# First attention: four query groups in one batch on 64-row halves, and a part of the keys' sums on ScalarE

## The chip, the cores and the metric

The kernel runs on one core of one Trainium2 chip. The metric is the device time of one execution in microseconds (us). The engines of the core work beside each other, each in the order of its own instructions, and wait for each other by semaphores: TensorE (PE in the profile; PEld is its loading of weights), VectorE (DVE), ScalarE (ACT), GpSimd (POOL) and SyncE (SP), which here only issues transfers (DMAs).

## The reference: two attentions and two MLPs in turn

The input x has 2048 tokens of 576 features, in bfloat16. Four layers are run, each added to x after a layer norm of its own: attention, MLP, attention, MLP, both attentions with the same weights and both MLPs too.

```python
qkv = (x @ wqkv) ...                      # 32 heads of 18 features
phi = lambda t: jnp.where(t > 0, t + 1, jnp.exp(t)) + 1e-6
pq, pk = phi(q), phi(k)
kv = jnp.einsum("bhsd,bhse->bhde", pk, v)
z = jnp.einsum("bhsd->bhd", pk)
num = jnp.einsum("bhqd,bhde->bhqe", pq, kv)
den = jnp.einsum("bhqd,bhd->bhq", pq, z)[..., None] + 1e-6
o = num / den                             # then o @ wo
```

The attention is linear: the keys and values are summed over all tokens into one small matrix per head, and the queries are multiplied with it. The MLP is 576 to 4608 with gelu and back; its input is normed twice, once by the layer and once inside.

## The kernel before

Tokens are in 16 tiles of 128; four tiles are a block of 512. The normed input is kept transposed in `yT`, five chunks of 128 features by 2048 tokens: four full chunks and a fifth with 64 features in its upper 64 rows; in the first attention the lower 64 rows of that chunk hold padding, against which the weights are zero. TensorE's order is the order in which the code calls `mm`, and the other engines are also held to the order of the code (the classes `InOrder` at L48 and the helper at L53, so that almost every row of the profile names L53 or L229).

**phi of a projection.** A projection lands in PSUM in float32. phi is computed as max(t, 0) + (min(exp(t), 1) + 1e-6). For a group of queries ScalarE reads PSUM twice (exponential and relu, 512 columns), and VectorE later clamps and adds the two in bfloat16 (`q_sum`). These sums are put in a list, `q_late`, and `finish(n)` does the oldest n of them.

**The key tiles of the first attention** (the loop over `t in range(NT)` in `layer_A`). At tile t TensorE transposes the normed tile t + 2, projects the keys of tile t + 1 in two halves (`k_half`, 288 columns, the second with 72 columns of values beside it), and between the matmuls of the second half does five small products with the sums `pk` of tile t (`m_side`); then four matmuls of 504 columns add the tile to the products of input and keys (`m_main`). ScalarE copies the transposed tile, takes the exponential of each half (`phi_e`) and copies the values. VectorE norms a tile further ahead, takes the statistics of one beyond that, and then does `k_finish`: for each half a clamp of `phi_e` (TENSOR_SCALAR) and a sum with the positive part, read from PSUM (SCALAR_TENSOR_TENSOR). GpSimd computes the reciprocal standard deviations and makes the masks, one batch a tile, each after that tile's last key sum. At seven tiles (1, 2, 3, 5, 7, 10, 14) one of the 18 query groups is projected between the second and the third of the four matmuls. PSUM banks one0, one1 and one2 go round among transposes, key halves and queries; the side products stay in one3.

**Behind the key tiles** the products are folded with the value and output weights (`kv_wo`), the first block's denominators are made, and five more query groups are projected. `kv_wo(4)` puts four small copies on SP. Then the output of the first block's four tiles is computed (`wo_stage`): VectorE adds it to x and takes the statistics of the next norm; ScalarE norms the first two tiles, VectorE the last two, and TensorE transposes them. Six query groups are projected among these: behind the first and the second output tile, and four after the last one, the very last with the fourth transposes between its second and third matmul. A query group (`q_next`, `q_proj`) is five matmuls of 128 rows by 512 columns; the fifth group of a pair of blocks, with 72 of the features, is 20 matmuls of 64 columns each way.

**The MLP's first matmuls follow.** `groups(2, ...)` runs two groups of the first MLP's hidden features for block 0, on the upper and the lower 64 rows of the array at the same time (`row_tiles`): each row half works on its own PSUM bank, and halves change banks in turns through a relay. Behind them come the denominators of the other blocks, which need all query sums.

**The second attention** (`placed` is true) has its rows placed by transfers, and ends in another way: its last four query groups are done by `q_batch`, in which each group is nine matmuls of 64 rows, four or five on each half of the array. For that the fifth chunk must lie on both halves of the rows, and the lower half's weights for it too: `lower_tails` copies them, on SP.

**Weights.** The list `late_pieces` holds 27 transfers on SP: output weights, value weights, nine of the MLP's first and two of their tails, two biases, and twelve of the MLP's second weights (432 KB each). `after_tile0` issues two of them at tile 1, one at tiles 2 to 10 and four at each tile from 11 on.

The lines that the change turns on:

```python
def k_finish(t):
    k_sum(t, 0)
    return k_sum(t, 1)
...
for _ in range(2 if t == 1 else 1 if t < NT - 5 else 4):
    if late_pieces:
        late_pieces.pop(0)()
```

Of the kernel before, what the change touches and what calls it, by code (L numbers as in the profile page):

```python
# [8 lines left out]
ALU = mybir.AluOpType  # L9
# [26 lines left out]
def build(tc, A_x, A_wqkv, A_wo, B_w1, B_b1, B_w2, B_b2, out, n_layers=4):  # L36
    nc = tc.nc
    with ExitStack() as ctx:
# [513 lines left out]
        def layer_A(li, next_kind, begin, before_tile, before_keys, mid_tile, rows_ahead, after_tile, q_tiles, placed, mlp):  # L552
# [3 lines left out]
            def k_half(t, half, beside=(), tag=None):  # L556
# [10 lines left out]
                act.activation(out=es[t][:, half * HALF:(half + 1) * HALF], in_=kp[:, 0:HALF], func=ACT.Exp)  # L567
                if half:
                    vas[t] = v_ring[t % NV]
                    act.copy(out=vas[t][:, 0:72], in_=kp[:, HALF:HALF + 72])  # L570
# [7 lines left out]
            def k_finish(t):  # L578
                k_sum(t, 0)
                return k_sum(t, 1)  # L580
# [29 lines left out]
            def q_proj(g, c, late, tag=None, between=None, evict=None):  # L610
# [19 lines left out]
                e = units[:, len(q_left) % (2 if placed else 4) if in_tiles[0] else (3 if placed else 4) + late_count(), :]  # L630
# [15 lines left out]
            def lower_tails():  # L646

                sp.dma_start(out=k_tail, in_=wkv_sb[0:64, 4, HALF:D + 72])
                sp.dma_start(out=q_tail, in_=wq_sb[0:64, 4, 0:4, :].rearrange("p (a b) c -> p a b c", b=2)[:, :, 1, :])

            def q_batch(es, tags):
# [13 lines left out]
                def after(n, done, turn):  # L665
# [5 lines left out]
                    act.activation(out=by_token(e, True), in_=as_read(dst[n][:], True), func=ACT.Exp)  # L671
                    vec.tensor_scalar(out=by_token(to, True), in0=as_read(dst[n][:], True), scalar1=0.0, scalar2=None, op0=ALU.max)
# [165 lines left out]
            for t in range(0 if placed else NT):  # L838
# [5 lines left out]
                if 1 < t < NT - 1:  # L844
                    k_half(t + 1, 0)
# [19 lines left out]
            in_tiles[0] = False  # L865
            if placed:
# [198 lines left out]
            kv_wo(4, act)  # L1065
            a, b = ("one1", "one0") if placed else ("one0", "one1")
# [12 lines left out]
            one_turn.update(n=3, banks=4)  # L1079

            for t in range(TPC):
# [5 lines left out]
                if t == 0 and not placed:  # L1087
                    finish(len(q_late) - 3)
                if t == 2:
                    first[1].norm()  # L1090
                if t < (1 if placed else 2):
                    q_next(True)
                if t == (3 if placed else 2):
# [4 lines left out]
            q_next(True, other[0] if placed else None)  # L1098
            first[1].transposed()
            q_next(True, other[1] if placed else None)  # L1100
# [3 lines left out]
            if placed:  # L1104
                finish(1)
            first[2].transposed()
            if placed:
                first[3].transposed((other[0],))
                finish(3)
                q_batch([units[:, i, :] for i in range(13, 17)], ("one2", "one1", "one3", other[1]))  # L1110
            else:
                q_next(True, other[1], first[3].transposed)
# [235 lines left out]
        def after_tile0(t, done):  # L1348
            for _ in range(2 if t == 1 else 1 if t < NT - 5 else 4):
# [69 lines left out]
```

## Time and profile before

| what | us |
|---|---|
| median of 3 runs (745.09 to 745.4) | 745.12 |
| the profiled execution | 745.02 |
| its span, first to last instruction | 743.3 |
| TensorE busy | 738.3 |
| VectorE / ScalarE / GpSimd busy | 272.0 / 295.2 / 132.2 |
| first key tile to the last (first to last load of pk's weights) | 10.8 to 56.5 |
| first output tile of the first attention | 67.41 |
| first matmul of the first MLP | 80.38 |
| denominators of the other blocks | 88.26 |
| first matmul of the MLP's second half | 130.0 |

The profile is of one execution. Its page shares the span out among engines and follows the chain that ended last back from the end; the timelines give, for each merged run of equal instructions, the start in us, its length, the engine, the line, the operation with the tiles it writes and reads, the shape, and how many there were; in brackets stands the idle time of the engine before it and what ended that. A matmul's length overlaps the next one's, so the time that a group takes is read from its start to the next start. TensorE's granted clock is 1.00 in every stretch of this trace that is cited.

### The profile page before, as it was taken

The page shows a single profiled execution, that of the slowest core. Times are in us where ns is not written, and L with a number is a line of the kernel's source. Part 1 is how long each engine was busy: PE and PEld are TensorE (multiplying, and loading weights), DVE is VectorE, ACT ScalarE, POOL GpSimd, SP SyncE. Part 2 cuts the span into 40 slices and gives each one's busy share as a digit, 9 for nine tenths or more (in the row PEclk, how much of TensorE's full clock was granted, in tenths as well). Part 3 has the DMA queues.
Part 4 walks back from the last instruction along what each step waited for, and adds up shares of the span by engine and source line. Part 5 has one row for each costly group of instructions (what it writes and reads, how often), then busy time and mean ns, then how long its engine had stood idle before and what let it go on. Part 6 is the DMA issues. An engine that isn't in the chain of part 4 may idle for free.

```text
span 743.3 us, 16635 instructions
## 1 busy us (share of the span) xinstructions
PE 738.3 (99%) x6935; PEld 477.3 (64%) x6935; DVE 272.0 (37%) x683; ACT 295.2 (40%) x633; POOL 132.2 (18%) x401
## 2 busy tenths in 40 slices
PE   8999999999999999999999999999999999999998
PEld 4666556774576457646777665777646754774476
DVE  8978635433124302400366685542401140100000
ACT  5657743007601740274035666320373047106700
POOL 4541100322022201200213120021200120010010
PEclk9999999999999999999999999999999999999999
DMA  8992020022011202110023101202000200020000
GB/s 201 232 353 78 4 92 11 15 47 44 2 27 41 37 2 41 40 26 1 17 81 86 31 1 37 67 1 52 17 2 9 53 10 1 17 44 10 1 12 21
DMA packets 61073, 34.64 MB, mean 47 GB/s; under 512 B 36966, under 2 KB 60998, under 8 KB 60998
## 3 DMA queue, kind: packets, MB, share of 16 engines
q1 hardware_dynamic: 60246, 33.35, 17.8%
q8 instruction: 54, 0.88, 0.5%
q10 hardware_dynamic: 752, 0.23, 0.1%
q14 instruction: 21, 0.17, 0.1%
HBM read 21.70 MB, written 4.93 MB: 36 GB/s over the span
## 4 chain that ended last, share of the span: by engine, by line
PE 98%; DVE 1%; DMA 1%; SPq 0%; issue 0%; DVEq 0%
PE m_ps L229 38%; PE hp_ps L229 21%; PE h_ps L229 17%; PE q_ps L229 5%; PE k_ps L229 5%; PE wo_ps L229 5%; PE rk_ps L229 4%; PE tp L468 1%; PE side_ps L229 1%; DMA x_sb<-in_A_x_dram 1%; SPq L53 0%; PE den_ps L229 0%; PE kvwo_ps L229 0%; PE kv_ps L229 0%; PE rden_ps L229 0%; DVE pk L53 0%
## 5 line engine op out<-in xcount | busy, mean ns | idle before, releaser
L229 PEld LDWEIGHTS <-units 128*128 128x128 bf16 (+1 forms) x2924 | 266.4, 97 | 67.1 <-issue 3.8
L229 PE MATMUL m_ps<-w_sb,units 128*128 128x288 bf16 (+2 forms) x2288 | 283.0, 286 | 0.0
L229 PEld LDWEIGHTS <-w_sb 64*128 64x128 bf16 x2304 | 128.4, 94 | 130.7 <-issue 2.3
L229 PE MATMUL h_ps<-yT,w_sb 64*128 64x512 bf16 x1152 | 174.6, 376 | 0.0
L229 PE MATMUL hp_ps<-yT,w_sb 64*128 64x512 bf16 x1152 | 150.8, 376 | 0.0
L53 DVE TENSOR_TENSOR x_sb<-m_ps,xo 128x576 bf16<-128x576 f32 (+3 forms) x34 | 24.4, 722 | 323.4 <-PE m_ps L229 323.4
L53 ACT ACTIVATE units<-hp_ps,b1T 128x512 bf16<-128x512 f32 x144 | 91.0, 683 | 86.1 <-PE hp_ps L229 86.1
L53 ACT COPY relay_sb<-relay_sb 128x1 f32<-128x1 f32 x112 | 21.4, 191 | 236.3 <-PE hp_ps L229 226.0
L53 ACT ACTIVATE units<-h_ps,b1T 128x512 bf16<-128x512 f32 x142 | 95.1, 686 | 0.0
L53 POOL TENSOR_TENSOR xo<-x_sb,b_bc 128x576 f32<-128x576 bf16 x32 | 40.8, 1274 | 302.8 <-DVE x_sb L53 291.4
L229 PE MATMUL k_ps<-wkv_sb,yT 64*128 64x288 bf16 (+3 forms) x432 | 61.0, 299 | 0.3 <-ACT yT L53 0.2
L229 PE MATMUL hp_ps<-yT,w_tail 64*128 64x512 bf16 x144 | 54.1, 376 | 0.0
L229 PE MATMUL h_ps<-yT,w_tail 64*128 64x512 bf16 x144 | 54.1, 376 | 0.0
L53 DVE BATCH_NORM_STATS2 ln_st<-x_sb 128x6 f32<-128x288 bf16 x128 | 51.3, 440 | 1.2 <-DMA x_sb<-in_A_x_dram 0.8
L53 ACT ACTIVATE phi_e<-k_ps 128x288 bf16<-128x288 f32 x64 | 26.3, 413 | 56.7 <-PE k_ps L229 53.0
L53 DVE STREAM_TRANSPOSE shared<-y_ring 128x640 bf16<-128x640 bf16 x40 | 32.9, 827 | 41.6 <-DMA yT<-shared 39.5
L229 PE MATMUL q_ps<-yT,wq_sb 128*128 128x512 bf16 (+2 forms) x268 | 42.8, 347 | 0.0
L229 PEld LDWEIGHTS <-yT 64*128 64x128 bf16 (+1 forms) x448 | 36.3, 95 | 8.9 <-ACT yT L53 0.5
L53 DVE TENSOR_SCALAR y_ring<-x_sb,ln_mv,ln_rstd 128x576 bf16<-128x576 bf16 (+2 forms) x60 | 31.0, 518 | 24.1 <-POOL ln_rstd L53 23.9
L53 ACT ACTIVATE units<-q_ps 128x512 bf16<-128x512 f32 x63 | 33.6, 608 | 13.2 <-PE q_ps L229 13.0
L53 POOL MEMSET pool_relay<- 128x1 f32 x150 | 16.6, 111 | 122.1 <-PE hp_ps L229 44.1
L229 PE MATMUL wo_ps<-shared,units 64*128 64x288 bf16 (+1 forms) x480 | 38.4, 283 | 0.0
(110 smaller groups left out, 494.2 us busy)
## 6 DMA issues: line engine op xcount, KB each, us to landing
yT<-shared SPq DMA_DIRECT2D x160, 40.0 KB
w_sb<-in_B_w_dram SPq DMA_DIRECT2D x12, 432.0 KB
w_sb<-in_B_w_dram SPq DMA_DIRECT2D x9, 512.0 KB
yT<-rden_rows SPq DMA_DIRECT2D x24, 126.0 KB
y_rows<-y_ring SPq DMA_DIRECT2D x16, 144.0 KB
units<-y_rows SPq DMA_DIRECT2D x16, 144.0 KB
x_sb<-in_A_x_dram SPq DMA_DIRECT2D x15, 144.0 KB
out_dram<-x_sb SPq DMA_DIRECT2D x15, 144.0 KB
```

The costliest lines, as they stand in the source:

```text
L53: inst = issue(*args, **kw)
L229: return pe(nc.tensor.matmul(out_, lhsT=lhsT, rhs=rhs, start=start, stop=stop, **kw))
L468: pe(nc.tensor.transpose(out=tp[:, k - a, :], in_=self.y[:, k * P:(k + 1) * P], identity=ident[:]))
```

## The change

It edits the first attention alone (`placed` false).

- Query groups at the key tiles: five in place of seven, at tiles 1, 2, 3, 8 and 14.
- Keys 3 to 15: ScalarE also takes the relu of the first half, from PSUM into `pk`. `k_finish` becomes one clamp over all 576 columns, one addition of the first halves in bfloat16, and the old sum for the second half alone.
- The end takes the order of the second attention: one query group behind the second output tile, three after the fourth, the first transposes a tile later; the late sums that stood behind the first output tile go behind those groups; the third and fourth transposes follow each other, and the last four groups (block 3, groups 0 to 3) are done by `q_batch`.
- `lower_tails` is called behind the key tiles; here it copies the fifth chunk's 64 features of block 3 to the lower rows of `yT`, over the padding, and the queries' weights as in the second attention.
- In `q_batch` the reordering of tokens depends on `placed`, and the buffers of the exponentials and the turn of PSUM banks are shifted to fit.
- Transfers: one of `late_pieces` at each tile from 2 on; the rest, eleven of the second weights, behind `kv_wo(4)`.

```diff
-            def k_half(t, half, beside=(), tag=None):
+            def k_half(t, half, beside=(), tag=None, relu=False):
...
                 act.activation(out=es[t][:, half * HALF:(half + 1) * HALF], in_=kp[:, 0:HALF], func=ACT.Exp)
+                if relu:
+                    act.activation(out=pks[t][:, half * HALF:(half + 1) * HALF], in_=kp[:, 0:HALF], func=ACT.Relu)
...
             def k_finish(t):
-                k_sum(t, 0)
-                return k_sum(t, 1)
+
+                e, pk = es[t], pks[t]
+                vec.tensor_scalar(out=e[:], in0=e[:], scalar1=1.0, scalar2=1e-6, op0=ALU.min, op1=ALU.add)
+                vec.tensor_tensor(out=pk[:, 0:HALF], in0=pk[:, 0:HALF], in1=e[:, 0:HALF], op=ALU.add)
+                return vec.scalar_tensor_tensor(out=pk[:, HALF:D], in0=kps.pop((t, 1))[:, 0:HALF], scalar=0.0,
+                                                in1=e[:, HALF:D], op0=ALU.max, op1=ALU.add)
...
-                e = units[:, len(q_left) % (2 if placed else 4) if in_tiles[0] else (3 if placed else 4) + late_count(), :]
+                e = units[:, (len(q_left) % 2 if placed else (len(q_left) + 2) % 4) if in_tiles[0] else (3 if placed else 4) + late_count(), :]
...
-                sp.dma_start(out=k_tail, in_=wkv_sb[0:64, 4, HALF:D + 72])
+
+                if placed:
+                    sp.dma_start(out=k_tail, in_=wkv_sb[0:64, 4, HALF:D + 72])
+                else:
+                    sp.dma_start(out=yT[64:P, 4, S - CA:S], in_=yT[0:64, 4, S - CA:S])
...
-                    act.activation(out=by_token(e, True), in_=as_read(dst[n][:], True), func=ACT.Exp)
-                    vec.tensor_scalar(out=by_token(to, True), in0=as_read(dst[n][:], True), scalar1=0.0, scalar2=None, op0=ALU.max)
+                    act.activation(out=by_token(e, placed), in_=as_read(dst[n][:], placed), func=ACT.Exp)
+                    vec.tensor_scalar(out=by_token(to, placed), in0=as_read(dst[n][:], placed), scalar1=0.0, scalar2=None, op0=ALU.max)
...
-                    k_half(t + 1, 0)
+                    k_half(t + 1, 0, relu=True)
...
             in_tiles[0] = False
+            if not placed:
+                lower_tails()
...
             kv_wo(4, act)
+            if not placed:
+                while late_pieces:
+                    late_pieces.pop(0)()
...
-            one_turn.update(n=3, banks=4)
+            one_turn.update(n=3 if placed else 0, banks=4)
...
-                if t == 0 and not placed:
-                    finish(len(q_late) - 3)
                 if t == 2:
                     first[1].norm()
-                if t < (1 if placed else 2):
+                if t == (0 if placed else 1):
                     q_next(True)
-                if t == (3 if placed else 2):
+                if t == 3:
                     first[0].transposed()
...
             q_next(True)
             first[2].norm()
-            q_next(True, other[0] if placed else None)
+            q_next(True, other[0])
             first[1].transposed()
-            q_next(True, other[1] if placed else None)
+            q_next(True, other[1])
             if placed:
                 q_next(True)
             first[3].norm()
-            if placed:
-                finish(1)
+            finish(1)
             first[2].transposed()
-            if placed:
-                first[3].transposed((other[0],))
-                finish(3)
-                q_batch([units[:, i, :] for i in range(13, 17)], ("one2", "one1", "one3", other[1]))
-            else:
-                q_next(True, other[1], first[3].transposed)
+            first[3].transposed((other[0],))
+            finish(3)
+            q_batch([units[:, i, :] for i in range(13, 17)], ("one2", "one1", "one3", other[1]))
...
-            for _ in range(2 if t == 1 else 1 if t < NT - 5 else 4):
+            for _ in range(2 if t == 1 else 1):
...
-                layer_A(li, nk, begin0, ..., after_tile0, (1, 2, 3, 5, 7, 10, NT - 2), False,
+                layer_A(li, nk, begin0, ..., after_tile0, (1, 2, 3, 8, NT - 2), False,
```

## The prediction, on record before the result

> **What bounds the kernel now.** I read the page's head and its chain first, to see whether any engine but TensorE can matter at all.
>
> ```profile
> span 743.3 us, 16635 instructions
> PE 738.3 (99%) x6935; PEld 477.3 (64%) x6935; DVE 272.0 (37%) x683; ACT 295.2 (40%) x633; POOL 132.2 (18%) x401
> PE 98%; DVE 1%; DMA 1%; SPq 0%; issue 0%; DVEq 0%
> ```
>
> TensorE carries 98% of the chain, so the change can win only matmul time, or a stall of TensorE, and it can lose by making one. Everything it edits lies in the first 88 us. I next took the table by stretches, for the key tiles.
>
> ```profile
> core 0: us, PE busy (x) PEld busy (x) DVE busy (x) ACT busy (x) POOL busy (x), PEclk, DMA share, GB/s
> 26.00:42.00 16.00, 16.00 (x150) 10.65 (x148) 14.80 (x46) 9.92 (x25) 9.92 (x26) 1.00 1.05 259
> ```
>
> In the key tiles TensorE is never idle (16.00 of 16.00) and its granted clock is full; VectorE is nearly full too (14.80). So there is no stall for the change to take away there, but VectorE's lateness is close. How close, the timelines of one tile without a query group say: ScalarE, VectorE, TensorE's weight loads, and the same loads one tile where no transposes come (tile 14).
>
> ```profile
> 40.48 0.41 ACT L53 ACTIVATE phi_e<-k_ps 128x288 bf16<-128x288 f32 x1 [0.48 <-PE k_ps L229]
> ...
> 41.10 0.23 DVE L53 TENSOR_SCALAR phi_e<-phi_e 128x288 bf16<-128x288 bf16 x1
> 41.46 0.46 DVE L53 SCALAR_TENSOR_TENSOR pk<-k_ps,phi_e 128x288 bf16<-128x288 f32 x1
> 41.83 0.42 DVE L53 TENSOR_SCALAR y_ring<-x_sb,ln_mv,ln_rstd 128x576 bf16<-128x576 bf16 x1
> ...
> 42.06 0.10 PEld L229 LDWEIGHTS <-pk 128*128 128x128 bf16 x1
> ...
> 53.03 0.46 DVE L53 SCALAR_TENSOR_TENSOR pk<-k_ps,phi_e 128x288 bf16<-128x288 f32 x1
> ...
> 53.52 0.10 PEld L229 LDWEIGHTS <-pk 128*128 128x128 bf16 x1
> ```
>
> The keys' sum pk is done at 41.46 + 0.46 = 41.92 and TensorE loads it at 42.06: 0.14 us of slack. In tile 14 it is done at 53.49 and loaded at 53.52: none.
>
> Last, the end of the first attention, and the end of the second, which already runs such a batch.
>
> ```profile
> 79.55 0.81 PE L229 MATMUL q_ps<-yT,wq_sb 128*128 128x512 bf16 x3
> 80.38 1.04 PE L229 MATMUL hp_ps<-yT,w_sb 64*128 64x512 bf16 x8
> ...
> 439.30 0.73 PE L468 MATMUL tp<-ident,y_ring 128*128 128x128 bf16 x10
> 439.96 2.11 PE L229 MATMUL q_ps<-yT,wq_sb 64*128 64x512 bf16 x17
> ...
> 443.86 1.03 PE L229 MATMUL hp_ps<-yT,w_sb 64*128 64x512 bf16 x8
> ...
> 444.96 0.82 PE L229 MATMUL h_ps<-yT,w_sb 64*128 64x512 bf16 x6
> ```
>
> The second attention's batch of four groups takes 439.96 to 443.86, 3.90 us. A single group takes 1.08 (77.48 to the transposes at 78.56).
>
> **The change part by part.** The sum is made against the profiled execution, 745.02 us (span 743.3 and 1.7 around it), 0.10 under the median of 745.12. 0.2% is 1.49 us, about what a measurement of this kernel can tell from no change: 743.63 to 746.61 is "within".
>
> *Two query groups leave the key tiles* (tiles 5, 7 and 10 lose theirs, 8 gets one): -2 x 1.08 = -2.16 us there, and the same comes back at the end. The 64-column group moves from tile 7 to 14 with its two mode gaps of 0.10. After the loop the group in PSUM bank one2 waits for that group's two evictions: 0.2 us of room (evictions would end at 57.4, the group starts at 57.6), so nothing.
>
> *The batch*: 3.90, and 0.10 ahead of it (the transposes end at 439.86), for 4 x 1.08 = 4.32: -0.32. It also covers the copy of the last transposed tile, for which the first MLP group waits now (three matmuls of 0.213 from 79.55 end at 80.19, the start is 80.38): -0.19. But in the second attention the MLP's second PSUM bank is late behind the batch (444.96 - 443.86 = 1.10, where the first attention has 81.26 - 80.38 = 0.88): +0.22.
>
> *The end of the attention, in its new order.* I lay it out on the clock of before, from the first output tile at 67.41. VectorE: two late query sums (70.88 to 72.30) go away, so the four residuals and statistics run at 69.10, 70.88, 72.64 and 74.36, and the last tile is normed 3.46 later, at 77.82 (before: 75.78 to 79.24). ScalarE: the second tile's norm can start 1.31 after its statistics (before: 74.15 to 75.46), at 74.03, but the tile-1 query group is evicted until 74.6; then norm and copy 1.04, transposed copy 0.59, a query's two evictions 0.96, another's 0.96: done at 78.2; transposed copy 0.57 and the third query's 0.96: 79.76. TensorE: output tiles and one group to 73.41, transposes to 73.81, two groups to 75.97, transposes 76.25, the 64-column group to 77.6, transposes to 77.9. The last transposes now write the bank of the second of those groups, so they wait for ScalarE until 78.26, about +0.35; they end at 78.54, and the batch starts at 78.64 (0.10 between, as at 439.96). Its fourth bank is that of the third group, wanted four pairs of matmuls (0.85) later, at 79.49, and free at 79.76: +0.3. The batch ends at 78.64 + 3.90 + 0.3 = 82.84; less the 2.16 saved earlier the MLP starts at 80.68 where it started at 80.38. **End of the attention, batch and covered copy included: +0.30, with the late bank +0.52.** The two waits for ScalarE in it, 0.65, are bounded by zero (-0.13 in place of +0.52) and by one more pair of evictions (0.96 more); I take them as the chain gives them. The nine query sums after the batch end 12.1 us behind its start in the second attention, and the denominators (451.95) do not wait visibly, so they add nothing.
>
> *The keys' sums.* ScalarE gets one more reading of 128x288 from PSUM, 0.41 in the second attention. It has 0.48 idle before the second exponential (the row at 40.48) and an instruction starts 0.31 after the one before (40.48 to 40.79), so it delays nothing. VectorE: two rounds of 0.23 and 0.46 become one clamp over 576, one addition of two bf16 rows and one round of 0.46; it gains some 0.35 us a tile, which TensorE, not waiting for it, does not see. But all three now come behind the second exponential, where two did. From its end, 40.89: start 0.03 (52.63 to 52.66 in tile 14); clamp 0.30 (0.23 for 288 and 0.28 for 512 elements, carried on to 576); 0.03 to the next; addition 0.25 until the next can start (388.64 to 388.89 in the second attention); 0.46; 0.03 to TensorE. Together 1.10: ready at 41.99, wanted at 42.06. So in the nine tiles without a query group (4 to 7 and 9 to 13): no stall, 0.07 of room. Bounds: below, nothing to gain; above, a clamp of 0.42 (the normalization's row at 41.83, the same width with scalars from memory), an addition of 0.42 (the 512-wide row) and two gaps of 0.13, as before 41.46: 1.62, a stall of 0.45 in each, 4.1 us. I take the lower, since immediates and 288 columns are nearer rows. **Tile 14** has no cover of transposes: 52.63 + 1.10 = 53.73 against 53.52, **+0.2**.
>
> *Transfers.* Eleven of the twelve second-layer weight pieces (432 KB) go behind the four small copies of the folded weights on SP, which end at 64.3. At the 352 GB/s that the same pieces reach between 42 and 58, 4.9 MB take 13.8 us, to some 78. Their first reader is at 130.0, the next transfer on SP is issued at 90.97: hidden, and uncovered only if they were 50 us late. The two tail copies stand on SP behind the last key tile and ahead of those four; nothing else is queued behind them, their reader is 20 us away, and the small copies wait for ScalarE at 61.6 anyway: nothing. The bias piece is issued at 37.97, ahead of all that moves: unchanged.
>
> **Sum:** 745.02 + 0.52 + 0.2 = 745.74, so **745.7**, 0.08% up: within 0.2%. Its own range is 745.0 to 746.5.
>
> **The rivals.** *Full gain.* ScalarE is in time for both banks and tile 14 hides: 745.02 - 0.13 = 744.9, and without the late bank 744.7. Against it: ScalarE's chain above, which has no idle time from 73.6 on. It cannot pass 0.2%: no row before 88 us has more than 0.7 us of TensorE's time in reach.
>
> *The other side: the key tiles become bound by ScalarE and VectorE in turn.* The place is the weight load at 42.06; the price is nine times what the chain is longer than 1.17. It decides from 0.10 a tile (746.61 - 745.74 = 0.87 over nine). For it: 0.07 is less than one gap of 0.13, which the second rounds show today (41.33 to 41.46). With one such gap (0.10 more) and a clamp of 0.36 (0.06 more) the chain is 1.26: 0.09 in each of nine tiles and 0.16 more in tile 14, 746.7. With the upper bounds it is 745.74 + 4.1 + 0.5 = 750.3. Against it: that gap follows a wait that here is over before the addition ends.
>
> *GpSimd in VectorE's way.* At 35.73 an addition of two 512-wide rows takes 0.75 us, not 0.43, while GpSimd runs a selection from 35.56 to 36.19. GpSimd's mask batches start 0.4 behind each sum and the largest take 1.46, so four of them now end about 0.2 into the next clamp: 3 x 0.2 to 4 x 0.2, 746.3 to 746.5. Against it: the clamp at 40.45 kept its 0.24 beside the selections of 39.30 to 40.76. The Trainium skill's page "SBUF — State Buffer", section "SBUF: two separate sides", has VectorE and GpSimd share one pair of ports under an exclusive lock, so that the later one waits for the whole of the other's instruction; by that rule each of the four overlaps costs a stall up to the selection's end. The row at 35.73 agrees with it, the one at 40.45 does not show it.
>
> **How the numbers follow.** The forecast 0.45; full gain 0.10; GpSimd 0.08; the key tiles bound 0.33, which is large because 0.07 us of room decides over nine tiles; something that no row shows and that makes it faster 0.04. Within 0.2%: 0.45 + 0.10 and 0.05 of GpSimd's, 0.60. Slower: the key tiles and the rest of GpSimd's, 0.36. Faster 0.04. The range reaches from just under the full gain (0.2 for the rounding of some twenty rows), 744.5, to nine tiles and tile 14 at 0.22 more than forecast, 745.74 + 2.2, 748.0.
>
> **What would show it.** The batch in 3.9 us and no group starting late after 81 us but the 1.10; clamps of 576 in 0.30; the weight loads of pk in tiles 4 to 7 and 9 to 13 still 2.66 us apart (longer by 0.1 or more: the other side); a gap of 0.2 in tile 14; the last transposes waiting for ScalarE. Wrong would make it a chain over 1.17 us, or a batch that waits longer than 0.3 for a bank.

## The result and the profile after

| | before | after |
|---|---|---|
| median of nine executions, us | 745.40 | 747.33 |
| lowest and highest | 745.09, 745.64 | 745.64, 748.45 |
| profiled execution: time, span | 745.02, 743.3 | 747.97, 746.2 |

The ratio is 1.0024, with a 95% interval of 1.0013 to 1.0034: slower by 0.24%, a little past the 0.2% that the prediction called measurable, while the interval reaches below it, to 0.13%. That is the outcome held at 0.36, though not for the reason that carried most of it. The range (744.5 to 748.0) holds the median; the likeliest case (745.7, 745.0 to 746.5) does not. That the range holds it is in part luck: its upper end was built from waits in the key tiles, and most of the loss came elsewhere. The scatter says as much as the median: before keeps within 0.55 us, after covers 2.8 us.

The head of the page after, and its chain by engine:

```profile
span 746.2 us, 16672 instructions
PE 738.9 (99%) x6951; PEld 475.9 (64%) x6951; DVE 272.0 (36%) x674; ACT 297.3 (40%) x642; POOL 132.2 (18%) x403
PE 94%; DVE 3%; ACT 1%; DMA 1%; POOL 1%; issue 0%; SPq 0%; DVEq 0%; POOLq 0%
```

TensorE's busy time grew by 0.6 us (738.3 to 738.9) and the span by 2.9, so some 2.3 us are added idle time; its share of the chain fell from 98% to 94%. Where the 2.9 us lie is read from the start of the same matmuls in both profiled executions:

| first matmul of | before, us | after, us | difference |
|---|---|---|---|
| first output tile (`wo_ps`) | 67.41 | 65.78 | -1.63 |
| MLP (`hp_ps`) | 80.38 | 80.88 | +0.50 |
| other denominators (`den_ps`) | 88.26 | 89.16 | +0.90 |
| outputs of block 1 (`wo_ps`) | 104.79 | 105.67 | +0.88 |
| second half of the MLP (`m_ps`) | 130.04 | 132.73 | +2.69 |
| the same, second layer pair | 493.61 | 496.39 | +2.78 |
| end of the span | 743.31 | 746.25 | +2.94 |

There are two losses: 0.9 us up to the denominators, and 1.8 us between 106 and 133 us, where the change edits nothing. First the second one. The chain of after in order of time there (start, duration, what):

```profile
107.68 3.33 DMA yT<-rden_rows
...
112.14 1.24 PE hp_ps L229 x9
```

The same place in the timeline, VectorE and then TensorE, of after:

```profile
107.70 1.43 DVE L53 TENSOR_TENSOR units<-yT,units 128x512 bf16<-128x512 bf16 x4 [4.88 <-DMA yT<-rden_rows]
111.14 0.29 DVE L53 TENSOR_TENSOR units<-yT,units 128x256 bf16<-128x256 bf16 x1 [2.00 <-DMA yT<-rden_rows]
111.34 2.87 DVE L53 TENSOR_TENSOR x_sb<-wo_ps,x_sb 128x576 bf16<-128x576 f32 x6
...
112.14 1.04 PE L229 MATMUL hp_ps<-yT,w_sb 64*128 64x512 bf16 x8 [1.69 <-DVE x_sb L53]
```

and of before:

```profile
108.44 0.29 DVE L53 TENSOR_TENSOR units<-yT,units 128x256 bf16<-128x256 bf16 x1 [0.20 <-DMA yT<-rden_rows]
...
109.46 1.04 PE L229 MATMUL hp_ps<-yT,w_sb 64*128 64x512 bf16 x8
```

VectorE multiplies block 2's queries by the reciprocals of their denominators, which transfers of SP have spread over the features (the spread): four scalings of 512 columns and a fifth of 256. Before, the fifth waits 0.20 us for its transfer and TensorE waits for nothing; after, it waits 2.00. Behind it in VectorE's order stand the additions of block 1's outputs (`x_sb<-wo_ps,x_sb`), and these free the PSUM banks that the next MLP group wants: TensorE waits 1.69 us, for `x_sb`. It is a wait for a transfer two steps back. Counted from the first denominator matmul, SP issues the last spread piece at 18.25 us before and at 18.52 after, and the fifth scaling starts at 20.18 and at 21.98: 0.27 us is late issue, the other 1.5 us is a slow landing.

What else was on the DMA engines? The profile's part on the DMA queues, from 108 to 110 us, ahead of the landing at 111.01, of after:

```profile
q8 instruction: 1, 0.02, 3.4%
```

A queue of the kind "instruction" moved one packet: 3.4% of 16 engines over 2 us is 1.09 us of one engine. Over the whole span that queue moves 54 packets and 0.88 MB, 16 KB each. TensorE has 6,951 matmuls and as many weight loads, 13,902 instructions: one packet for every 256, so I read it as the fetch of TensorE's program. The packet starts 19.55 us behind the denominators' first matmul; the corresponding one of before starts at 21.0, when the fifth scaling (20.18) has begun. The change has 16 more matmuls and 16 more weight loads ahead of this point.

The times of the single packets show how the two meet. The last two pieces of block 2 (27 and 5 KB) are 64 rows of 512 bytes. Before, all are through at 19.47 us behind the denominators' first matmul. After, 63 are through at 19.85, and the last one moves from 20.62 to 20.70, as the instruction packet ends (20.64): below, such a row is called held. The fifth scaling starts 1.28 us behind that row, against 0.71 behind the last row before; why that distance grows too is not shown.

The first loss. The timeline of after for one key tile without a query group (VectorE, GpSimd, then TensorE's weight loads; the last line is one tile later):

```profile
42.61 0.26 DVE L53 TENSOR_SCALAR phi_e<-phi_e 128x576 bf16<-128x576 bf16 x1
...
43.69 0.94 DVE L53 TENSOR_SCALAR y_ring<-x_sb,ln_mv,ln_rstd 128x576 bf16<-128x576 bf16 x1
...
43.09 0.57 POOL L53 TENSOR_TENSOR ln_rstd<-ln_u,neg_half 128x1 f32<-128x1 f32 x1
43.65 1.40 POOL L53 TENSOR_SCALAR_AFFINE_SELECT head_bc<-head_bc 128x504 bf16<-128x504 bf16 x4
...
46.53 0.10 PEld L229 LDWEIGHTS <-pk 128*128 128x128 bf16 x1 [0.27 <-issue]
```

The normalization takes 0.94 us where it took 0.42 (41.83 in the timeline of before): it starts 0.04 behind a mask selection of GpSimd. Everything of VectorE behind it is late, so the next tile's keys' sum is late too, and TensorE waits 0.27 for it at 46.53. Four waits for VectorE, behind the matmuls that start at 37.23, 40.54, 43.26 and 46.16, come to 0.68 us.

The end of the attention in the timeline of TensorE, after:

```profile
76.48 0.44 PE L468 MATMUL tp<-ident,y_ring 128*128 128x128 bf16 x5 [0.25 <-ACT units L53]
76.85 2.24 PE L229 MATMUL q_ps<-yT,wq_sb 64*128 64x512 bf16 x17
...
80.88 1.22 PE L229 MATMUL hp_ps<-yT,w_sb 64*128 64x512 bf16 x8
...
82.16 1.04 PE L229 MATMUL h_ps<-yT,w_sb 64*128 64x512 bf16 x8
```

The last transposes wait for ScalarE; the batch takes 4.03 us (76.85 to 80.88); the MLP's second bank comes 1.28 us behind the first.

### The profile page after: what moved, and what is told of

It reads as the page before. It is cut to its first block, busy times and chain, and to the rows that moved or that the text cites. A ratio compares the mean times of both kernels' runs of the same rounds, so it can differ in the third digit from the quotient of the medians.

```text
span 746.2 us, 16672 instructions
## 1 busy us (share of the span) xinstructions
PE 738.9 (99%) x6951; PEld 475.9 (64%) x6951; DVE 272.0 (36%) x674; ACT 297.3 (40%) x642; POOL 132.2 (18%) x403
## 4 chain that ended last, share of the span: by engine, by line
PE 94%; DVE 3%; ACT 1%; DMA 1%; POOL 1%; issue 0%; SPq 0%; DVEq 0%; POOLq 0%
PE m_ps L229 38%; PE hp_ps L229 20%; PE h_ps L229 17%; PE k_ps L229 4%; PE q_ps L229 4%; PE wo_ps L229 4%; PE rk_ps L229 3%; DVE ln_st L53 1%; DVE y_ring L53 1%; PE side_ps L229 1%; ACT units L53 0%; PE tp L468 0%; DVE units L53 0%; DMA yT<-rden_rows 0%; POOL ln_rstd L53 0%
## 5 line engine op out<-in xcount | busy, mean ns | idle before, releaser
L53 DVE TENSOR_SCALAR y_ring<-x_sb,ln_mv,ln_rstd 128x576 bf16<-128x576 bf16 (+2 forms) x60 | 33.3, 557 | 24.5 <-POOL ln_rstd L53 24.0
L229 PE MATMUL q_ps<-yT,wq_sb 64*128 64x512 bf16 (+2 forms) x282 | 41.9, 349 | 0.0
L229 PEld LDWEIGHTS <-w_tail 64*128 64x128 bf16 x288 | 27.1, 94 | 16.9
```

What stands on the lines that cost most here:

```text
L53: inst = issue(*args, **kw)
L229: return pe(nc.tensor.matmul(out_, lhsT=lhsT, rhs=rhs, start=start, stop=stop, **kw))
```

## The experiments

Two theories. **Theory 1**: the mask selections hold up the normalization, and once a tile is late the next one is too. **Theory 2**: the fetch packet meets the last spread pieces of block 2. Rivals are in each expectation. All times are medians with the lowest and highest execution; the kernel before had 745.08 beside the first four kernels, 745.20 beside the next four and 745.01 beside the last four, each with 23 to 30 executions.

**The changed kernel again.**

> The changed kernel once more, beside the three others and the kernel before. Both of my theories expect what it showed: a median 1 to 2.5 us over the kernel before, with executions spread over 2 us or more where the kernel before spreads over 0.6. Theory 1 (GpSimd's mask selections hold up VectorE's normalization in tiles 8 to 11): again about 0.7 us of waits of TensorE between 36 and 47 us, behind normalizations of 0.9 us instead of 0.42. Theory 2 (a 16 KB packet of the instruction queue, which fetches TensorE's program, runs beside the last transfers that spread the reciprocals of block 2, and delays them): in this profile too the packet starts 19 to 20 us behind the first denominator matmul, and the first matmul behind the fifth scaled piece waits between 0 and 2 us, by another amount than 1.69. Rival for the second: if the wait is again 1.7 to within 0.1 and the times are as wide, the packet's chance position is not what varies.

Measured: 747.71 (746.42 to 750.25), ratio 1.0036, interval 1.0025 to 1.0046. Its profiled execution (746.42) differs from the one above in both places. In block 2 TensorE waits 0.23 us instead of 1.69, with the packet at the same place (19.63) but no row held (all 64 are through at 19.89), and in the second attention 0.42. In the key tiles there is no wait at all; the timeline of the same tile (VectorE, GpSimd, weight loads):

```profile
43.05 0.42 DVE L53 TENSOR_SCALAR y_ring<-x_sb,ln_mv,ln_rstd 128x576 bf16<-128x576 bf16 x1
44.77 0.31 DVE L53 TENSOR_SCALAR phi_e<-phi_e 128x576 bf16<-128x576 bf16 x1 [0.33 <-ACT phi_e L53]
45.12 0.31 DVE L53 TENSOR_TENSOR pk<-pk,phi_e 128x288 bf16<-128x288 bf16 x1
45.34 0.45 DVE L53 SCALAR_TENSOR_TENSOR pk<-k_ps,phi_e 128x288 bf16<-128x288 f32 x1
...
42.29 0.57 POOL L53 TENSOR_TENSOR ln_rstd<-ln_u,neg_half 128x1 f32<-128x1 f32 x1
43.20 1.46 POOL L53 TENSOR_SCALAR_AFFINE_SELECT head_bc<-head_bc 128x504 bf16<-128x504 bf16 x4 [0.34 <-DVE pk L53]
...
45.90 0.10 PEld L229 LDWEIGHTS <-pk 128*128 128x128 bf16 x1
```

Here the normalization (43.05) starts 0.15 ahead of the selection (43.20) and takes 0.42. So the same program has two courses in tiles 9 to 12, called locked and free below; the MLP starts at 80.88 in the one profile and at 80.25 in the other. In the locked one the normalization waits for the reciprocal deviation that GpSimd has just finished (43.09 + 0.57 = 43.66), and GpSimd goes straight on to the selection; in the free one that value is there (42.29 + 0.57 = 42.86) 0.19 before the normalization starts. The theory's expectation that the lock comes each time fell.

**Mask batches later** (the four `head_bc` selections in tiles 12 to 15).

```diff
-            if 2 <= t < 2 + len(batches):
-                first = batches[t - 2]()
+            n = t - 2 if t < 8 else t - 6
+            if t >= 2 and not 8 <= t < 12:
+                first = batches[n]()
```

> The changed kernel with the four largest mask batches of GpSimd moved from key tiles 8 to 11 to key tiles 12 to 15, where no normalization is left. Theory 1 (the shared lock): every normalization of 576 columns in 0.42 to 0.45, TensorE's waits between 36 and 47 us gone, its tiles 2.66 apart, the denominators about 0.7 earlier than in the changed kernel; the median lower by about 0.7 if nothing else moves. Rival (the longer chain of ScalarE and VectorE itself is what TensorE waits for, as the prediction's second rival had it): the tiles 8 to 11 stay 2.7 to 2.9 apart and nothing is won. By theory 2 the spread of the times stays as wide as in the changed kernel, since the packet's place relative to the denominators does not change.

Measured: 747.91 (746.36 to 748.60). The normalizations from tile 8 on take 0.42, the tiles are 2.77 (less the query group's 1.08), 2.66, 2.66 and 2.66 us apart (2.77, 2.72, 2.90, 2.90 in after), the denominators come at 88.77 instead of 89.16. TensorE never waited for the chain of ScalarE and VectorE, so that rival falls. What stays is 0.11 us in tile 9, from an earlier normalization of 1.35 us beside GpSimd's fill of `head_bc` at tile 7. The median is no lower; the profiled execution has a wait of 1.89 us in block 2, with a row held until 20.89 (the packet ends at 20.83).

**The fetch moved in the changed kernel, by 54 instructions.**

```diff
-        warm(NWARM - 1)
+        for i in range(36):
+            mm(warm_ps[:, 0:128], y_ring[NY - 1][:, 0:P], y_ring[NY - 1][:, 0:128], True, True)
```

> The changed kernel with its nine warm-up matmuls of 512 columns written as 36 of 128 columns, the same columns in all, in time that TensorE would idle anyway. TensorE's program has 54 instructions more ahead of everything else, so each fetch of 16 KB (256 instructions) comes 54 instructions earlier, some 2.9 us in the MLP. Theory 2 (the fetch beside the spread of block 2): the packet now starts about 16.6 us behind the first denominator matmul instead of 19.5, ahead of the last pieces, the wait of 1.7 us goes or falls under 0.3, the executions agree within 0.8 us, and the median is 1 to 1.8 us under the changed kernel's, 745.6 to 746.3. Theory 1 is untouched: the 0.7 us between 36 and 47 stays. Rival (the spread is late because the batch or the moved weight pieces disturb it): no change from the changed kernel, 747 with a spread of 2 us.

Measured: 746.93 (746.47 to 747.75). The packet moved to 17.1 us (18.65 in the second attention), the wait fell to 0.38, but the second attention has 0.49, and the times lie 1.3 us apart instead of the expected 0.8. Partly as expected: no long waits, but the median missed.

**The fetch moved in the kernel before, by 28 instructions.**

```diff
-        warm(NWARM - 1)
+        for i in range(23):
+            mm(warm_ps[:, 0:200], y_ring[NY - 1][:, 0:P], y_ring[NY - 1][:, 0:200], True, True)
```

> The kernel before with its nine warm-up matmuls of 512 columns written as 23 of 200 columns: 28 instructions more of TensorE ahead of everything else, nothing else changed. Theory 2: the fetch that starts 21.0 us behind the first denominator matmul in the kernel before now starts at about 19.5, where it stands in the changed kernel; so the kernel before becomes slower by 0.5 to 1.8 us in the median and its executions spread over 1.5 us or more, though its attention is untouched. Rival (the changed attention itself delays the spread): the same 745.4 as before, within 0.3, with executions within 0.6 us.

Measured: 747.00 (745.03 to 747.21), ratio 1.0014, interval 1.0005 to 1.0023. The eleven executions stand in two groups: 745.03, 745.07, 745.13, 745.17, 745.44 and 747.00, 747.02, 747.09, 747.18, 747.21, 747.21. The profiled one (745.07) is of the lower group: packet at 19.49, TensorE waits 0.14. No operation of the attention was touched; 28 instructions at the start, in time that TensorE waits through anyway, made six executions in eleven 2.0 us slower. Of the times alone, this is the strongest evidence for theory 2; none of the six was profiled, so where in them the 2.0 us lie is not shown.

**Each part of the change alone.** The keys' sums alone, on the kernel before: of the change's diff, the `relu` of `k_half`, its call, and

```diff
             def k_finish(t):
-                k_sum(t, 0)
-                return k_sum(t, 1)
+                e, pk = es[t], pks[t]
+                vec.tensor_scalar(out=e[:], in0=e[:], scalar1=1.0, scalar2=1e-6, op0=ALU.min, op1=ALU.add)
+                vec.tensor_tensor(out=pk[:, 0:HALF], in0=pk[:, 0:HALF], in1=e[:, 0:HALF], op=ALU.add)
+                return vec.scalar_tensor_tensor(out=pk[:, HALF:D], in0=kps.pop((t, 1))[:, 0:HALF], scalar=0.0,
+                                                in1=e[:, HALF:D], op0=ALU.max, op1=ALU.add)
```

> The kernel before with the keys' sums of the change alone (ScalarE's relu, one clamp, one addition, one round from PSUM); its query groups, batch and transfers stay. TensorE's program has not one instruction more, so theory 2 expects the fetch at 21.0 us behind the first denominator matmul as before, no wait in block 2, and executions within 0.8 us. Theory 1: if the lock is entered in tiles 8 to 11, up to 0.7 us more, as a second value of the same kernel; if not, nothing. Median 745.1 to 745.8. Rival (the new chain of three operations is itself longer than the cover): 0.05 to 0.2 us in each of the tiles without a query group, the same in all executions, 745.6 to 747.

Measured: 745.32 (744.88 to 745.77), ratio 1.0002, interval 0.9993 to 1.0011. They cost nothing: the normalizations take what they took before, and the packet is at 21.5. In the profiled execution (745.70) TensorE still waits 0.36 in block 2: the spread has no room there even without a fetch beside it.

The query groups, the batch and the transfers alone (the changed kernel with that diff turned round, and `k_half(t + 1, 0)` without `relu=True`):

> The changed kernel with the keys' sums of before: the query groups, the batch, the late transfers alone. Theory 2: the fetch stands at 19.5 us behind the first denominator matmul, as in the changed kernel, so the executions spread over 2 us and the median lies 1 to 2.5 us over the kernel before, 746.2 to 747.6. Theory 1: no normalization over 0.5 us beside a selection in tiles 9 to 12. Rival (the new keys' sums are what costs): the kernel before's time, within 0.5.

Measured: 747.76 (746.14 to 750.20), ratio 1.0030, interval 1.0019 to 1.0040: the whole loss. No normalization from tile 9 on is over 0.42. The profiled execution is the slowest (750.20), with the packet at 19.99, a row held until 21.00 (the packet ends at 20.95) and 2.00 us of wait. And something else; the table by stretches (columns as in the prediction, PEclk the granted clock):

```profile
114.00:118.00 4.00, 4.00 (x26) 1.89 (x24) 2.55 (x8) 0.34 (x1) 0.20 (x2) 0.61 0.10 30
118.00:122.00 4.00, 4.00 (x67) 3.45 (x64) 1.26 (x3) 2.08 (x4) 0.29 (x3) 1.00 0.00 0
```

The granted clock is half for some 3.1 of the 4 us from 114 to 118 (by the clock's own record, from 113.70 to 117.12): the pairs of matmuls start 0.427 us apart, not 0.217. From the denominators to the second half of the MLP it takes 3.79 us longer than before, 2.00 of wait and 1.8 of slow matmuls. That would explain the three executions at 750, two here and one of the changed kernel: their mean granted clock is on record as 0.998, 0.998 and 0.997, and as 0.999 or 1.0 for all others of these two kernels. Only this one has a profile.

**Much longer warm-ups**, 126 instructions more, and the same with the masks later by the diff above.

```diff
-        warm(NWARM - 1)
+        for i in range(72):
+            mm(warm_ps[:, 0:64], y_ring[NY - 1][:, 0:P], y_ring[NY - 1][:, 0:64], True, True)
```

> The changed kernel with its nine warm-up matmuls of 512 columns written as 72 of 64: 126 instructions of TensorE more ahead of everything else. Theory 2: the fetch moves on from 17.1 (36 warm-ups) to about 13.5 us behind the first denominator matmul, and in the second attention to about 14: long before the last pieces of block 2 are issued at 18. Left is only that the spread of block 2 is issued 0.27 us later than before, a wait of 0.2 to 0.4; none in the second attention (0.49 with 36 warm-ups). Median 745.5 to 746.2 (the upper end with theory 1's lock), executions within 0.9 us. Rival (the place of the fetch does not matter, only some other effect of longer warm-ups): 746.9 as with 36.

> The same 72 warm-ups, and the four mask batches in tiles 12 to 15. By theory 1 the lock cannot be entered behind tile 9: at most 0.1 us of waits in the key tiles, so this is at or under the 72 warm-ups alone, by 0 to 0.6 us in the median, and narrower: 745.4 to 745.7. Rival (the masks at their new place hold up other work of VectorE in tiles 13 to 15): 0.1 to 0.4 us over the 72 warm-ups alone.

Measured: 747.30 (746.95 to 748.31) and 746.79 (746.38 to 748.08); both medians missed. The profiled executions say why. In the first, the packets are at 13.6 and 15.1, and the waits in block 2 are 0.11 and 0, as theory 2 said; but a query group at 14.6 us waits 0.52 for its weights, and the key tiles are locked. In the second no tile is locked, and the waits are 0.51 and 0.05 with the packets at 13.3 and 15.9. So with no fetch of TensorE's program near, 0.1 to 0.5 us of wait remains; the late issue is 0.27 of it at most, and the rest is not explained. One more thing lies near: a packet of 8 KB of a second instruction queue, at 18.4 and 18.9 us here, which the change moved as well (12.25 before, 18.45 after). It is not what makes the long waits: the query groups alone have none near the last pieces and wait 2.00 us.

**The scalings behind the additions.** If the additions are late only because they stand behind the fifth scaling, their order can be turned: block 2 is needed 3 us later.

```diff
             groups(4)
-            scales(2)
             outputs(1)
+            scales(2)
             groups(1)
```

> The changed kernel with VectorE's five scalings of block 2 issued behind the additions of block 1's outputs instead of ahead of them, in both attentions; nothing else, so the fetch of TensorE's program stays at about 19.5 us behind the first denominator matmul, beside the last spread pieces. Theory 2, with its second half (the fifth scaling waits for the late piece, and the additions that free TensorE's PSUM banks stand behind it in VectorE's order): the piece may come as late as before, but TensorE no longer waits for it; no gap at the first MLP group behind the outputs, the distance from the denominators to the second half of the MLP is that of the kernel before, 41.7 to 41.8. Median 745.4 to 746.1 (theory 1's lock makes the difference), executions within 0.9 us, none over 747. Rival (the wait has another cause than the late piece): still 747 to 748 with a spread of 2 us.

Measured: 746.03 (745.32 to 746.82), ratio 1.0011, interval 1.0002 to 1.0019. The timeline of VectorE and TensorE:

```profile
111.92 1.63 DVE L53 TENSOR_TENSOR units<-yT,units 128x512 bf16<-128x512 bf16 x5
...
110.27 1.07 PE L229 MATMUL hp_ps<-yT,w_sb 64*128 64x512 bf16 x8
```

The scalings run at 111.92 with nothing to wait for, TensorE starts the group at 110.27 without a wait, and the denominators are 41.71 and 41.65 us ahead of the second half of the MLP (before: 41.78 and 41.66). The packets are at 20.2 and 19.6, beside the spread as they were, but no row was held in this execution (all are through at 20.01); the last experiment has a profile with one. The executions lie within 1.5 us of each other (0.9 expected), half of the changed kernel's 2.8, and none is over 747. What is left is the first loss: key tiles locked in the profiled execution, MLP 0.52 later, denominators 0.92 later.

**The fetch put where it was**, with 228 instructions more, as good as 28 fewer.

```diff
-        warm(NWARM - 1)
+        for i in range(123):
+            at = 32 * (i % 4)
+            mm(warm_ps[at:at + 32, 0:P], y_ring[NY - 1][:, 0:32], y_ring[NY - 1][:, 0:P], True, True, skip_group_check=True)
```

> The changed kernel with its nine warm-up matmuls of 512 columns written as 123 with 32 columns of weights: 228 instructions of TensorE more, which with 256 to a fetch is as good as 28 fewer. Theory 2: the fetch stands where it stands in the kernel before, about 21 us behind the first denominator matmul (21.8 in the second attention), behind the last pieces. What is left of the wait is 0 to 0.5 us, from the spread being issued 0.25 us later; no execution with a wait of 1.7 or more, median 745.5 to 746.5, if the start is not delayed. Rival: the changed kernel's times, 747 to 748 with a spread of 2 us.

Measured: 747.89 (747.37 to 748.15, five executions). The packets stand at 21.2 and 21.7, as in the kernel before, and the waits are 0.22 and 0.31: no long one, and the times are within 0.8. But a key tile waits 0.79 at the start for its weights, so the median says nothing for itself.

**Later transfers in the kernel before.**

```diff
             heads, to = rden_rows[c], spare(c)
+            if c == 2 and not placed:
+                for i in range(5):
+                    sp.dma_start(out=late_rows[i:i + 1, :], in_=ident[i:i + 1, :])
```

> The kernel before with five small transfers (one row of 256 bytes each, to a scratch array) put ahead of the spread of block 2 on SP in the first attention; they take 0.45 to 0.65 us each to issue, so the pieces come 2.2 to 3.2 us later. If the fifth scaling sets TensorE's first MLP group behind the outputs with no room, TensorE waits 2.2 to 3.2 us there and the time rises at least by that, to 747.3 to 748.3. If, further, a wait of 2 us or more makes the granted clock fall (one profile of the query groups alone shows 2.00 us of wait, then 3.3 us at half pace), the time rises by another 1.8, to 749.1 to 750.1, and the stretch of 4 us behind the wait shows a clock of about 0.6. Rival (the clock fell there for another reason): the clock stays at 1.00 and the time under 748.4.

Measured: 747.25, 747.39, 749.79, 750.32, 750.46, 750.84. The last spread piece is issued 1.74 later (19.99 instead of 18.25), which is most of the 2.3 us by which the lower pair is over the kernel before. In the profiled one (749.79), VectorE's fifth piece, TensorE, and the stretch behind:

```profile
112.31 0.29 DVE L53 TENSOR_TENSOR units<-yT,units 128x256 bf16<-128x256 bf16 x1 [2.29 <-DMA yT<-rden_rows]
...
113.32 1.04 PE L230 MATMUL hp_ps<-yT,w_sb 64*128 64x512 bf16 x8 [3.56 <-DVE x_sb L53]
```

```profile
112.00:116.00 4.00, 2.68 (x26) 1.45 (x27) 3.69 (x10) 0.00 (x0) 0.20 (x2) 1.00 0.31 102
```

The wait is 3.56, 1.8 more than the later issue; the packet, at 21.7 (21.0 in the kernel before), now lies beside the last pieces, and one of their rows is held until 22.59 (the packet ends at 22.54). Here the transfers were pushed to the packet, with the 23 warm-ups the packet to the transfers, and both give two groups of times. The other half of the expectation is open: in the profiled execution the clock stays at 1.00 behind a wait of 3.56 us, but the three slowest, 750.32 to 750.84, have a mean granted clock of 0.997 or 0.998 on record, the other three of 1.0.

**Three things at once**: the scalings behind, the masks later (both diffs above), and another first bank.

```diff
-            one_turn.update(n=3 if placed else 0, banks=4)
+            one_turn.update(n=3, banks=4)
```

> The changed kernel with the scalings of block 2 behind the additions, the four mask batches in tiles 12 to 15, and the MLP's first PSUM bank taken one earlier in the ring (the first group in the bank that the batch does not use). Theory: no wait in block 2, no lock in the key tiles, and the first group's second bank late by 0.2 instead of 0.4: MLP start as in the kernel before or 0.13 earlier, denominators 0.1 to 0.3 later, end 0.16 later: 745.1 to 745.4, executions within 0.6 us, the same as the kernel before. Rivals: the bank order does nothing (745.4 to 745.6), or the second bank is then late by more (over 745.6).

Measured: 746.56 (746.42 to 747.23). No wait in block 2, no lock, and without the profiled execution, which starts 0.6 late, the times are within 0.4 us. In that profile a row is held until 20.74 (the packet ends at 20.69), and TensorE does not wait: with the additions ahead of the scalings, the late piece costs nothing. But the bank order is wrong: the line of TensorE shows the second group of the MLP waiting for VectorE's evictions of the batch,

```profile
83.48 1.02 PE L229 MATMUL h_ps<-yT,w_sb 64*128 64x512 bf16 x7 [1.05 <-DVE units L53]
```

so the MLP's start to the denominators takes 9.28 us, against 8.28 in after and 7.88 before. Less that 1.0, it would be some 745.6, worked out and not measured. No version here beats the kernel before.

## Why the prediction was right or wrong

The forecast was 0.7 us over the profiled execution of before; the scalings-behind kernel, which has everything of the change but the wait in block 2, is 1.0 over. The range held, but one step failed, which the prediction did not price: it followed TensorE, ScalarE and VectorE to the denominators, let the query sums end there ("so they add nothing"), and under *Transfers* counted only what the change moves. The transfers it should have looked at were not moved: the 0.20 us of wait in front of the fifth scaling and no wait at `hp_ps` 109.46 say that block 2 had no room at all.

- **Two query groups leave the key tiles (-2.16).** Right: -2.26 at the first output tile in the free course (65.15).
- **The batch and the end of the attention (+0.30).** 4.03 us for the batch against 4.2 with its wait; the last transposes started some 0.42 late (0.25 of it shows as idle), against 0.35. From the first output tile to the MLP it took 15.10 us, 15.43 by the forecast's layout, so the MLP starts 0.13 earlier than before in the free course (80.25), not 0.30 later. The +0.50 of the other course, equal to the forecast's +0.30 and +0.20, is a coincidence: the lock made up for the two waits.
- **The late second bank (+0.22).** Mis-sized: the second bank comes 1.28 behind the first, not 1.10, and the MLP's start to the denominators takes 0.40 more.
- **The keys' sums (no stall).** Right, to the operation: in the free course the second exponential ends at 44.74, and clamp, addition and round end at 45.79, 1.05 later (1.10 forecast), loaded at 45.90. Clamp 0.31 (0.30), addition 0.22 until the next starts (0.25), round 0.45 (0.46). The rival that these tiles become bound by this chain, held at 0.33, fell.
- **Tile 14 (+0.2).** Wrong: the row of matmuls there is as long as before (0.76 against 0.77). That the first loads read only the half of the sum that is ready earlier is argued from the code, not shown.
- **GpSimd in VectorE's way (0.08).** The mechanism was right, the place wrong: not the clamp, but the normalization behind it. The price is 0 or 0.68, by how the tiles 7 and 8 went, against 0.6 to 0.8. The keys' sums made VectorE early enough to meet GpSimd; with query groups in tiles 5, 7 and 10 as before the new sums cost nothing. The Trainium skill's page "SBUF — State Buffer", section "SBUF: two separate sides", says that, of a GpSimd operation and a VectorE operation that needs the shared pair of ports, whichever starts first gets the pair for its whole instruction. Both courses agree (0.94 behind a selection, 0.42 ahead of it).
- **Transfers (nothing).** True for the weight pieces: nothing waits for them. Not true for the spread, above.
- **The end.** The last 0.16 us lies behind the last matmul: SP's closing wait for the last output is the third of five waits before and the first of five after, and the short ones follow it. The prediction had no term for it.

Sum for the profile of the scalings behind: 0.92 at the denominators (0.40 late bank, 0.65 lock, counted from the free course's MLP start, less 0.13 won), less 0.08 from there to the second halves of both MLPs, and 0.16 at the end, 1.00 in all; its execution took 746.03, 1.01 over 745.02.

What stays open: why a row is held in one execution and not in another at the same distance. Five profiles have one: those with the waits of 1.69, 1.89, 2.00 and 3.56 us, and the one with three things at once; the other nine have none. Five more times, a row of an earlier piece moves as a packet of 8 KB of the second instruction queue ends (at 18.93 in the changed kernel's second profile). Presumably such a row shares a DMA engine with the packet, but the trace does not record the engine.

## What to carry to other kernels

Ask of each stage that the change does not touch how much room its waits have: a stage with none turns any shift, even of code, into time. Where an engine's instruction waits for a transfer, look what stands behind it in that engine's order, and issue first what others wait for; here two exchanged lines took the long waits out. When the executions of a kernel spread wider than before, profile it twice: the one profile showed the lock and the long wait, the other neither.

## What the runs showed of the hardware

- TensorE's program comes by DMA, 16 KB for every 256 instructions and, as the held rows suggest, on the DMA engines that move the kernel's data; 0.9 to 1.5 us a packet in these traces. Adding 28 instructions at the start moved the one beside the spread by 1.5 us, and made six executions in eleven 2.0 us slower.
- GpSimd and VectorE can settle into one of two courses for several tiles with the same program; the waits of the locked one come to 0.68 us, the free one has none.
- A row of 512 bytes can be held up to the end of an instruction packet, 0.8 to 1.3 us behind the other rows of its piece (five profiles).
- The clock fell to half for 3.41 us behind a wait of 2.00 us, and in the profile with a wait of 3.56 not at all. The traces suggest that what counts is how the wait falls on steps of 3.413 us: in every trace with a clock record, the clock keeps a value for a whole multiple of that, up to the end of the program (216 of them in the kernel before, 217 after, 32 and then 1 with the query groups alone). On these steps the wait of 2.00 us falls into one, in which TensorE is busy for 1.41 us, and the next step is at half. The wait of 3.56 is shared by two steps, with 1.6 to 1.7 us busy in each, and the 1.69 of the changed kernel leaves 1.72 busy; the clock stays full. So the limit would lie between 1.41 and 1.6 us of 3.413, read from one fall. The Trainium skill's page "TensorE: Matmul & The Clock Gate", section "What's actually happening", has the clock halve after at least one idle window of about 3.4 us, and says that the windows run freely. The steps of 3.413 us agree with it; that the window has to be idle throughout does not, since TensorE was busy for 1.41 us of it.
- The order in which the end of the program waits for its DMA queues shifts with the number of transfers: 0.16 us here. The kernel before issues 337 and has the long wait third of five, the changed one issues 339 and has it first; with five more than before, 342, it is third again.
